# Where a fused RWKV-7 and feed-forward kernel begins its feed-forward, and who fetches its first weights

## The chip, the cores and the metric

The kernel runs on one NeuronCore of a Trainium2 chip. The core has five engines with a program each: TensorE (PE in the profile, its weight loads PEld), VectorE (DVE), ScalarE (ACT), GpSimd (POOL) and SyncE (SP). Each engine takes its instructions in the order of the program and waits on semaphores for the others. Transfers are issued by an instruction in the program of SP, ACT or POOL and are carried by 16 DMA engines that all of these share; an issuing instruction that has to wait (for a buffer, or for the data that it is to store) holds up everything behind it on its engine. The metric is the device time of one execution in microseconds, 1203.58 us before the change as the median of three runs (1201.11 to 1208.3).

## The reference, cut to what matters

```python
# r, k, v, w, a, b: (4 batches, 8 heads, 768 steps, 40), float32
for t in range(768):
    y[:, :, t] = einsum('bhd,bhde->bhe', r_t, state)
    Sa         = einsum('bhde,bhe->bhd', state, a_t)
    state      = state * w_t[:, :, None, :] - einsum('bhd,bhe->bhde', Sa, b_t)
    state      = state + einsum('bhd,bhe->bhde', v_t, k_t)
x = y.transpose(0, 2, 1, 3).reshape(3072, 320)
h = maximum(x @ w_in, 0)            # w_in  (320, 2048), float64
out = (h * h) @ w_out               # w_out (2048, 320), float64
```

The two feed-forward matrices come as float64. The kernel reads them as pairs of 32-bit words and makes float32 of them itself; that is called rounding below.

## The kernel before, in words

**Chunks and slots.** The 768 steps are cut into 6 chunks of 128 for each of 4 batches, 24 chunks in all, in the order of `order` (the four batches of one chunk in turn). The main loop (line 755) has one turn per chunk, called a slot here. Slot i interleaves, step by step (`weave`, 12 steps), up to five generators: `chain(i)`, the part of chunk i that depends on the state; `rest(i + 1)`, which turns and scales k, r, v, b of the next chunk; `prepare(m)` (`early`, with its loads) for a chunk 4 to 8 slots ahead, one or two of them in slots 0 to 15; 12 steps of the feed-forward `second`; and, in slots 0 to 3, some steps of `rounded`. The order in which these generators are stepped is the order of the program on every engine.

**The triangular solves.** `early` builds a triangular system per chunk and stores it to DRAM (`kept_q`, `kept_d`, `kept_n`, `kept_m`) together with the decays (`kept_e`, 780 KB). GpSimd solves the systems in units of two or four chunks: `solve(u)` loads a unit (`half_n`), takes 31 or 63 steps of a multiplication and a subtraction (lines 420 and 422), and stores the result (`kept_t`). `inverses(i)` reads the result back as T. For the first four chunks, whose systems are solved in halves, it also joins the halves: a transpose on DVE (line 454), small matmuls and copies in two steps. Chunk i of a unit cannot go through `chain(i)` before its unit is solved.

**Loads.** `load(i)` (line 148) issues, on SP's queue, the decays of the chunk (from slot 1 on) and then k, r, v and b, each 160 KB in pieces of 160 bytes. `load_early(i)` issues w, b and a for `early`. A store or a later load is put in `line` by `later(fn, steps)` and issued after so many steps.

**Rounding.** The raw words arrive in 21 fetches: 5 of 1 MB for `w_in` (two pieces of 512 columns each) and 16 of 320 KB for `w_out` (one piece each), 26 pieces in all. A piece takes two steps of `rounding`: two ACT operations (lines 257 and 261) and five DVE operations (lines 274 to 276, 265 and 266). The raw words lie where space is still unused: in `w_out` itself as long as it isn't filled (`wide`, `tails`), in the feed-forward's `hidden` (`lent`), and in two buffers of their own. `then` says after which piece which fetch is issued, on SP's queue; the first three (13 transfers) are issued on ACT's queue at line 711, right after the first solve.

**The feed-forward.** `ffn()` takes two chunks (256 tokens) as a group, 24 steps each. Eight pairs of blocks of 128 hidden units (16 steps, "in" below): for each block two 128-row matmuls and one 64-row matmul into `ps_f` (two buffers), then ACT's Relu (line 624) and DVE's product (line 625), which frees the buffer. Then 8 steps of four matmuls with `w_out` ("out"). A group's in steps wait for 10 finished pieces, its out steps for all 26. `share` says how many steps a slot runs before its chain and inside it: 6 before slot 2 and 2 inside, 8 inside slot 3, 4 before slot 4, 12 inside from slot 4 on. What is left after slot 23 runs alone at the end, 28 of 288 steps.

**Before the main loop** (lines 705 to 745, the prelude) the first two chunks are prepared and solved, chunks 2 and 3 prepared, chunk 0 taken through `rest`, and five pieces begun.

## Time and profile before

| | |
|---|---|
| median of three runs | 1203.58 us (1201.11 to 1208.3) |
| the profiled execution | 1197.18 us, span of its instructions 1195.5 us |
| busy share of the span | PE 85%, PEld 67%, DVE 40%, ACT 19%, POOL 57% |
| mean granted TensorE clock | 0.892 of full speed |
| moved by DMA | 114.38 MB in 260837 packets, 242828 of them under 512 B |
| queue of SP / of ACT / of POOL | 92.33 / 3.54 / 17.30 MB |

All times of a profile are microseconds from the start of the span of one profiled execution. In a timeline row the columns are start, duration, engine, source line, operation, output<-input, shape and count; the bracket at the end gives how long the engine had been idle and what ended that. SPq, ACTq and POOLq are the engines' own issuing of transfers. In a row of a table by stretches, each engine's busy time stands with its number of instructions, then the granted clock, the mean busy share of the DMA engines and GB/s.

### The profile page before, as it was taken

The numbers are of one execution on the slowest core, as the hardware profiler recorded it, in microseconds if no ns is written. First come the engines' busy times: TensorE is split into PE (matmuls) and PEld (weight loads), VectorE is DVE, ScalarE is ACT, GpSimd is POOL, SyncE is SP. The second block draws the span as 40 slices with busy tenths as digits, with TensorE's granted clock in tenths as the row PEclk, the third lists the DMA queues.
The fourth block names the chain that finished last, engine by engine and source line by source line (L and its number), as shares of the span: only waits on it lengthen the run. The fifth ranks groups of instructions, "written<-read, shape, count | busy, mean of one in ns | idle before, by whom it ended". The sixth has DMA issues, their size and how long they took to land.

```text
span 1195.5 us, 18978 instructions
## 1 busy us (share of the span) xinstructions
PE 1017.6 (85%) x7504; PEld 801.3 (67%) x7504; DVE 481.1 (40%) x1002; ACT 230.2 (19%) x535; POOL 683.7 (57%) x1112
## 2 busy tenths in 40 slices
PE   4248548858998999889979999879999999999898
PEld 3237446746776777667757777667777778777676
DVE  5347557636344246154144354142433132332211
ACT  2033222311121112112112112112122121221211
POOL 3753288458818866999279991179995881000000
PEclk9757557778999879979989989988999999999999
DMA  7894836372565947614565434544235433404000
GB/s 94 172 169 108 173 83 122 97 132 64 95 149 83 186 122 119 133 50 68 155 106 92 92 72 110 139 88 74 64 72 119 93 62 68 78 4 90 1 17 12
DMA packets 260837, 114.38 MB, mean 96 GB/s; under 512 B 242828, under 2 KB 248972, under 8 KB 258956
## 3 DMA queue, kind: packets, MB, share of 16 engines
q1 hardware_dynamic: 256476, 92.33, 39.9%
q0 software_dynamic: 2576, 17.30, 5.8%
q10 hardware_dynamic: 1696, 3.54, 1.3%
q8 instruction: 59, 0.97, 0.4%
q14 instruction: 30, 0.25, 0.1%
HBM read 76.42 MB, written 34.74 MB: 93 GB/s over the span
## 4 chain that ended last, share of the span: by engine, by line
PE 66%; DVE 13%; DMA 8%; SPq 7%; issue 3%; ACT 2%; ACTq 0%; DVEq 0%
PE ps_f L87 31%; PE ps_c L87 19%; PE ps_w L87 11%; SPq L142 4%; DMA in_k<-in_k_dram 3%; PE ps_w L314 3%; DVE decay L355 2%; SPq L108 2%; DVE hid L625 2%; DVE decay L356 2%; DMA in_w<-in_w_dram 1%; PE ps_w L512 1%; DVE RV L330 1%; PE ps_c L565 1%; ACT hid L624 1%
## 5 line engine op out<-in xcount | busy, mean ns | idle before, releaser
L420 POOL TENSOR_TENSOR half_p<-half_n,half_t 128x252 f32<-128x252 f32 (+52 forms) x503 | 306.7, 610 | 125.7 <-DMA half_n<-kept_d 66.7
L422 POOL TENSOR_TENSOR half_t<-half_t,half_p 128x252 f32<-128x252 f32 (+52 forms) x503 | 336.0, 668 | 39.4
L87 PE MATMUL ps_f<-tokens,w_in 128*128 128x256 f32 x704 | 206.1, 420 | 22.0 <-DVE hid L625 17.1
L87 PE MATMUL ps_f<-w_out,hid 128*128 128x320 f32 x704 | 205.7, 440 | 2.4 <-DVE hid L625 1.9
L87 PEld LDWEIGHTS ps_f<-w_out,hid 128*128 128x128 f32 x704 | 129.6, 192 | 52.3 <-DVE hid L625 4.9
L87 PEld LDWEIGHTS ps_f<-tokens,w_in 128*128 128x128 f32 x704 | 129.1, 203 | 49.1 <-DVE hid L625 27.1
L625 DVE TENSOR_TENSOR hid<-ps_f,hid 128x256 f32<-128x256 f32 x176 | 65.7, 414 | 238.0 <-ACT hid L624 238.0
L624 ACT ACTIVATE hid<-ps_f 128x256 f32<-128x256 f32 x176 | 57.9, 381 | 188.4 <-PE ps_f L87 188.3
L408 POOL DMA_DIRECT2D half_n<-kept_d x22 | 10.9, 500 | 121.3 <-DMA kept_d<-N 105.4
L488 DVE TENSOR_TENSOR kvT<-ps_w,dec 128x512 f32<-128x512 f32 x24 | 16.2, 675 | 126.8 <-PE ps_w L314 126.8
L87 PE MATMUL ps_f<-tokens,w_third 64*128 64x256 f32 x352 | 66.2, 455 | 0.0
L87 PEld LDWEIGHTS ps_c<-xr,T 64*64 64x64 f32 x768 | 53.2, 146 | 18.6 <-issue 16.7
L351 DVE TENSOR_TENSOR_SCAN decay<-ps_w,ones 128x64 f32<-128x64 f32 x88 | 23.5, 267 | 98.9 <-PE ps_w L314 98.9
L87 PE MATMUL ps_c<-xr,T 64*64 64x40 f32 x768 | 59.0, 238 | 1.1 <-ACT xr L547 1.0
L87 PEld LDWEIGHTS ps_c<-in_v,A 128*128 128x128 f32 x384 | 51.5, 210 | 2.7 <-issue 0.3
L87 PE MATMUL ps_w<-dec,kvT 40*128 40x128 f32 x384 | 35.1, 324 | 20.4 <-ACT N L367 11.8
L87 PE MATMUL ps_c<-in_v,A 128*128 128x40 f32 x384 | 50.4, 295 | 0.0
L87 PEld LDWEIGHTS ps_f<-tokens,w_third 64*128 64x128 f32 x352 | 28.3, 197 | 32.0 <-issue 31.0
L87 PE MATMUL ps_w<-rT,xnT 40*128 40x128 f32 x384 | 37.5, 320 | 14.3 <-DVE RV L330 13.5
L87 PEld LDWEIGHTS ps_w<-rT,xnT 40*128 40x128 f32 x384 | 30.8, 216 | 25.0 <-DVE RV L330 20.0
L87 PEld LDWEIGHTS ps_w<-dec,kvT 40*128 40x128 f32 x384 | 29.7, 221 | 25.5 <-ACT N L367 12.0
L367 ACT COPY N<-ps_w 128x512 f32<-128x512 f32 x48 | 25.8, 589 | 100.0 <-PE ps_w L87 60.5
(149 smaller groups left out, 1406.5 us busy)
## 6 DMA issues: line engine op xcount, KB each, us to landing
kept_e<-decay SPq DMA_DIRECT2D x22, 780.0 KB
dec<-kept_e SPq DMA_DIRECT2D x22, 780.0 KB
half_n<-kept_d POOLq DMA_DIRECT2D x16, 384.0 KB, 9.8
half_n<-kept_d POOLq DMA_DIRECT2D x6, 768.0 KB, 10.7
in_w<-in_w_dram SPq DMA_DIRECT2D x24, 160.0 KB
in_ab<-in_b_dram SPq DMA_DIRECT2D x24, 160.0 KB
in_ab<-in_a_dram SPq DMA_DIRECT2D x24, 160.0 KB
in_k<-in_k_dram SPq DMA_DIRECT2D x24, 160.0 KB
```

The source lines that it names most:

```text
L87: nc.tensor.matmul(o, l_, r_, start=start, stop=True, skip_group_check=True)
L108: later(lambda: queue.dma_start(out=out_, in_=in_), steps)
L142: nc.sync.dma_start(out=t_[:, :, :D], in_=src[bb, :, c * C:(c + 1) * C, :].rearrange("h t d -> t h d"))
L314: nc.tensor.transpose(p_[:, q * 128:(q + 1) * 128], pair(x_, q), ident)
L351: nc.vector.tensor_tensor_scan(up[:, q, MID + 1:C + 1], wT[:, q, MID:], ones, 1.0, Alu.mult, Alu.mult)
L355: nc.vector.reciprocal(down[:, :, MID + 1:C + 1], up[:, :, MID + 1:C + 1])
L356: nc.vector.reciprocal(up[:, :, :MID], down[:, :, :MID])
L367: nc.scalar.copy(t_[:, e * NP:(e + 1) * NP], p_)
L420: nc.gpsimd.tensor_tensor(p_, part[:, at:at + m_].unsqueeze(1).to_broadcast([128, n, m_]), t3[:, :n, s:s + 1].to_broadcast([128, n, m_]), ...
L422: nc.gpsimd.tensor_tensor(t3[:, :n, s + 1:], t3[:, :n, s + 1:], p_, Alu.subtract)
L624: nc.scalar.activation(h_, p_, Act.Relu)
L625: nc.vector.tensor_tensor(h_, p_, h_, Alu.mult)
```

## The change

Six things are altered.

1. The first three fetches of raw weights are issued by GpSimd instead of ACT: two ahead of its first solve, the third behind it.
2. Raw words of `w_out` lie in five places in turn (two own, three in `hidden`) instead of seven in a fixed list; `tails` goes, the list `then` is shorter, the first fetches of `w_out` are issued earlier and each later one when the piece that had its place is finished. A piece's `mant` and `bits` are both in PSUM (`ps_f`).
3. `load` issues k first, then the decays, then r; v and b follow two steps later.
4. `inverses` of a chunk is begun in `rest` where it was, but its joining steps are done at the end of `rest`; its two halves of small products lie in two PSUM tiles instead of one. In the prelude the joining of chunks 0 and 1 is begun right behind the second solve.
5. In a pair of blocks the two 64-row products come first, and a step ends after each block instead of after the first block's 128-row products and after the pair.
6. No feed-forward step runs in slots 0 to 3; 8 run before slot 4. Rounded pieces per slot are 4, 6, 6, 6 instead of 4, 8, 5, 5. After slot 23, 40 steps are left.

```diff
@@ -146,10 +146,12 @@
         early_loaded[i] = {nm: fetch(ring, src, i) for nm, ring, src in (("w", "w", w), ("b", "ab", b), ("a", "ab", a))}
 
     def load(i, g=None):
+        x_ = loaded[i] = {"k": fetch("k", k, i)}
         if g is not None:
             g["dec"] = new("dec", [128, 3, NP, C + 2], 2)
             nc.sync.dma_start(out=g["dec"], in_=kept_e[i])
-        loaded[i] = {nm: fetch(nm, src, i) for nm, src in (("k", k), ("r", r), ("v", v), ("b", b))}
+        x_["r"] = fetch("r", r, i)
+        later(lambda: x_.update(v=fetch("v", v, i), b=fetch("b", b, i)), 2 if g is not None else 0)
 
     load_early(0)
     load_early(1)
@@ -201,7 +203,6 @@
     lowest = single("lowest", [128, 1])
     nc.vector.memset(lowest, -896.0 * (1 << 23))
     wide = [room[:, 4 * WI * i:4 * WI * (i + 1)] for i in range(2)] + [free_words[:, :4 * WI]]
-    tails = [room[:, NF * DM - 2 * DM * (i + 1):NF * DM - 2 * DM * i] for i in range(2)]
     lent = [free_words[:, 2 * DM * i:2 * DM * (i + 1)] for i in range(3)]
     own_ = [single(f"raw{i}", [128, 2 * DM]) for i in range(2)]
 
@@ -228,14 +229,12 @@
               [w_third[:, WI * i:WI * (i + 1)] for i in range(2)])
     NARROW = len(pieces)
     WIDE = len(fetches)
-    in_turn = [own_[0], own_[1], tails[0], lent[0], lent[1], lent[2], tails[1], own_[0], own_[1], tails[0], tails[1],
-               own_[0], own_[1], own_[0], own_[1], own_[0]]
+    in_turn = [*own_, *lent]
     for f in range(NF):
-        fetchable(in_turn[f], [(0, 128, moe_w_out[f * 128:(f + 1) * 128, :])], [w_out[:, f, :]])
-
-    then = {0: (), 1: (3,), 3: (4,), 5: (5,), 6: (6,), 7: (8,), 8: (9,), 9: (7, 10)}
-    then.update({NARROW + n: tuple(WIDE + m_ for m_ in ms) for n, ms in
-                 ((0, (6, 7)), (1, (8,)), (2, (9,)), (6, (10,)), (7, (11,)), (8, (12,)), (11, (13,)), (12, (14,)), (13, (15,)))})
+        fetchable(in_turn[f % 5], [(0, 128, moe_w_out[f * 128:(f + 1) * 128, :])], [w_out[:, f, :]])
+
+    then = {0: (WIDE,), 1: (3,), 2: (WIDE + 1,), 3: (4,), 5: (WIDE + 2, WIDE + 3), 6: (WIDE + 4,)}
+    then.update({NARROW + f: (WIDE + f + 5,) for f in range(NF - 5)})
     finished = [0]
     left = lambda: len(pieces) - finished[0]
 
@@ -253,7 +252,7 @@
         for n in range(len(pieces) + 1):
             before, now = now, None
             if before:
-                _, _, _, bits = before
+                bits = before[-1]
                 nc.scalar.activation(bits, bits, Act.Relu, bias=lowest, scale=float(1 << 23))
             if n < len(pieces):
                 dst, raw = pieces[n]
@@ -268,9 +267,9 @@
                 for m_ in then.get(n - 1, ()):
                     later(lambda m_=m_: fetch_weights(m_, nc.sync), 1)
             if n < len(pieces):
-                hi, mant = words[:, :, 1].bitcast(I32), words[:, :, 0]
-                m_ = dst.shape[-1]
-                bits = (psum(ps_f)[:, :m_] if n < NARROW else new("bits", [128, DM], 1)).bitcast(I32)
+                hi = words[:, :, 1].bitcast(I32)
+                bits, mant = (psum(ps_f)[:, :dst.shape[-1]] for _ in range(2))
+                bits = bits.bitcast(I32)
                 nc.vector.tensor_scalar(bits, hi, 20, 0x7FF, Alu.logical_shift_right, Alu.bitwise_and)
                 nc.vector.tensor_scalar(mant.bitcast(I32), hi, 0xFFFFF, 0x100000, Alu.bitwise_and, Alu.bitwise_or)
                 nc.vector.tensor_tensor(mant, mant.bitcast(I32), dst, Alu.add)
@@ -454,20 +453,22 @@
         nc.vector.transpose(upper_.rearrange("p h t -> p (h t)"), blocks.rearrange("p h t -> p (h t)"))
         for n in range(2):
             nc.scalar.activation(T[:, :, n * Q:(n + 1) * Q], blocks, Act.Copy, scale=which[:, n:n + 1])
-        p_ = psum(ps_w).rearrange("p (n h t) -> p n h t", n=2, h=H)
+        small = lambda: psum(ps_w)[:, :H * Q].rearrange("p (h t) -> p h t", h=H)
+        p_ = small()
         mv = spare("mv", i)
         ends_ = [(slice(half * HC, half * HC + Q), slice(half * HC + Q, (half + 1) * HC)) for half in range(2)]
         for one, two in ends_:
             for h in range(H):
-                mm(p_[two, 0, h], g["joins"][one, h], upper_[one, h], True)
+                mm(p_[two, h], g["joins"][one, h], upper_[one, h], True)
         for one, two in ends_:
-            nc.scalar.copy(mv[two], p_[two, 0])
-        yield
+            nc.scalar.copy(mv[two], p_[two])
+        yield
+        p_ = small()
         for one, two in ends_:
             for h in range(H):
-                mm(p_[one, 1, h], mv[two, h], blocks[two, h], True)
+                mm(p_[one, h], mv[two, h], blocks[two, h], True)
         for one, two in ends_:
-            nc.scalar.copy(T[one, :, Q:], p_[one, 1])
+            nc.scalar.copy(T[one, :, Q:], p_[one])
         yield
 
 
@@ -487,11 +488,14 @@
         yield
         nc.vector.tensor_tensor(kT, kT_, down[:, :, 1:C + 1], Alu.mult)
         nc.vector.tensor_copy(ends, down[:, :, 0])
-        if soon(i) and i > 1:
-            yield from inverses(i, g)
+        joining = inverses(i, g) if i > 1 else iter(())
+        if soon(i):
+            next(joining, None)
         yield
         g["A"] = masked("A", 4, kT, aT)
         yield
+        while "v" not in x_:
+            line.pop(0)[1]()
         nc.scalar.copy(rT, turn(x_["r"]))
         vT = turned("kvT", 1)
         nc.scalar.copy(vT, turn(x_["v"]))
@@ -523,8 +527,7 @@
             sd = g["sd"] = new("sd", [128, NP, 2, DP], 2)
             nc.scalar.copy(sd.rearrange("p q e d -> p q (e d)"), quads(p_))
         yield
-        if not soon(i):
-            yield from inverses(i, g)
+        yield from joining
         yield
 
 
@@ -612,19 +615,16 @@
             for f in range(0, NF, 2):
                 ps = [psum(ps_f if gi < len(order) // GB - 1 else ps_w)[:, :GB * C] for _ in range(2)]
                 for e, p_ in enumerate(ps):
+                    half = slice(e * DP, (e + 1) * DP)
+                    mm(p_, w_third[half, f * 64:f * 64 + 128], t_[half, NT, :], True)
+                for e, p_ in enumerate(ps):
                     for j in range(NT):
-                        mm(p_, w_in[:, j, (f + e) * 128:(f + e + 1) * 128], t_[:, j, :], j == 0)
-                    if e == 0:
-                        yield True
-                for e, p_ in enumerate(ps):
-                    half = slice(e * DP, (e + 1) * DP)
-                    mm(p_, w_third[half, f * 64:f * 64 + 128], t_[half, NT, :], False)
-                for e, p_ in enumerate(ps):
+                        mm(p_, w_in[:, j, (f + e) * 128:(f + e + 1) * 128], t_[:, j, :], False)
                     h_ = hidden[:, (gi * NF + f + e) % (NF + 1)]
                     nc.scalar.activation(h_, p_, Act.Relu)
                     nc.vector.tensor_tensor(h_, p_, h_, Alu.mult)
                     hid.append(h_)
-                yield True
+                    yield True
             while left():
                 yield False
             for n in range(GB):
@@ -704,12 +704,15 @@
 
     run(firsts(0, 2))
     flush()
+    if moe_w_in.dtype != FP32:
+        for n in range(2):
+            fetch_weights(n, nc.gpsimd)
     solve(0, [nc.sync, nc.scalar])
     load_early(3)
     if moe_w_in.dtype != FP32:
-        for n in range(3):
-            fetch_weights(n, nc.scalar)
+        fetch_weights(2, nc.gpsimd)
     load(0)
+    flush()
     rounded = rounding() if moe_w_in.dtype != FP32 else as_they_are()
     e2, e3, r0 = early(2), early(3), rest(0, ready[0])
     go(e2, 3)
@@ -718,27 +721,27 @@
     go(r0, 3)
     flush()
     load(1)
+    flush()
     go(e3)
     go(r0)
     go(rounded, 2)
     go(e3, 2)
+    flush()
+    solve(1, own)
+    joined = [inverses(i, ready[i]) for i in range(2)]
+    go(joined[0])
+    go(joined[1])
     go(rounded)
     go(r0)
-    flush()
-    solve(1, own)
     go(rounded, 2)
     go(r0)
     go(rounded, 3)
-    tc.no_sync_barrier()
-    joined = [inverses(i, ready[i]) for i in range(2)]
-    go(joined[0])
-    go(joined[1])
     load_early(B)
     go(r0, 3)
-    go(rounded, 2)
     for _ in range(2):
         go(joined[0])
         go(joined[1])
+    go(rounded, 2)
     for gen in (e2, e3, r0, *joined):
         run(gen)
     flush()
@@ -748,8 +751,8 @@
     TOTAL = STEPS // GB
     ahead = {0: (4, 5), 1: (6,), 2: (7,), 3: (8,), 4: (9,), 5: (10, 11), 6: (12, 13), 7: (14, 15)}
     ahead.update({i: (i + 8,) for i in range(8, len(order) - 8)})
-    share = {0: (0, 0), 1: (0, 0), 2: (2, 6), 3: (8, 0), 4: (TOTAL, 4)}
-    pieces_in = {0: 4, 1: 8, 2: 5, 3: 5}
+    share = {**{i: (0, 0) for i in range(B)}, B: (TOTAL, 8)}
+    pieces_in = {0: 4, 1: 6, 2: 6, 3: 6}
     done = set(range(B))
     unit = FINE
     for i in range(len(order)):
```

## The prediction

> **What bounds the kernel now.** I read the chain of waits first, then a table of the engines by stretches, then the start of every slot, then single waits in the early slots.
>
> ```profile
> span 1195.5 us, 18978 instructions
> PE 66%; DVE 13%; DMA 8%; SPq 7%; issue 3%; ACT 2%; ACTq 0%; DVEq 0%
> ```
> ```profile
> 0.00:94.00 94.00, 38.48 (x306) 32.64 (x307) 42.81 (x85) 19.55 (x39) 51.87 (x151) 0.73 0.86 144
> 94.00:130.00 36.00, 27.19 (x240) 24.16 (x239) 32.46 (x62) 11.76 (x22) 8.01 (x22) 0.74 0.38 102
> 130.00:201.00 71.00, 40.25 (x311) 33.45 (x310) 37.54 (x68) 15.76 (x36) 53.39 (x94) 0.62 0.67 135
> 201.00:238.00 37.00, 33.38 (x291) 28.82 (x289) 26.30 (x52) 12.23 (x29) 20.99 (x44) 0.68 0.33 88
> 238.00:303.00 65.00, 47.20 (x307) 37.70 (x306) 30.63 (x61) 11.54 (x27) 49.13 (x88) 0.82 0.53 110
> 303.00:588.00 285.00, 264.42 (x1933) 208.31 (x1932) 121.71 (x258) 51.40 (x120) 205.85 (x316) 0.90 0.55 111
> 588.00:1118.00 530.00, 494.62 (x3761) 385.69 (x3759) 178.58 (x391) 96.56 (x233) 294.45 (x400) 0.97 0.41 84
> ```
>
> From 303 us on TensorE is busy for 264 of 285 and 495 of 530 us: there the kernel is bound by matrix work, which the change does not reduce. The first 303 us are another matter: PE works 38 of 94 us in the prelude and 148 of 209 in slots 0 to 3, at 0.62 to 0.82 of its clock, and the chain runs through DVE, DMA and SP's queue. So the change is decided there. I count a slot from its first copy into xr:
>
> ```profile
> 93.85 0.42 ACT L547 COPY xr<-ps_c 64x320 f32<-64x320 f32 x1 [2.77 <-PE ps_c L87]
> ...
> 129.10 0.42 ACT L547 COPY xr<-ps_c 64x320 f32<-64x320 f32 x1 [1.20 <-PE ps_c L87]
> ...
> 200.22 0.42 ACT L547 COPY xr<-ps_c 64x320 f32<-64x320 f32 x1 [1.26 <-PE ps_c L87]
> ...
> 236.95 0.42 ACT L547 COPY xr<-ps_c 64x320 f32<-64x320 f32 x1 [1.65 <-PE ps_c L87]
> ...
> 302.40 0.42 ACT L547 COPY xr<-ps_c 64x320 f32<-64x320 f32 x1 [4.37 <-PE ps_c L87]
> ...
> 587.56 0.42 ACT L547 COPY xr<-ps_c 64x320 f32<-64x320 f32 x1 [4.42 <-PE ps_c L87]
> ```
>
> Slots 0 to 3 take 35.3, 71.1, 36.7 and 65.5 us (208.6 in all); the last row is the start of slot 10. I forecast against the profiled execution's own time, 1197.2 us; the median of the runs lies 6.4 above it, and that is added at the end.
>
> **First weights by GpSimd; joining early (prelude).** The timeline, then the group of the solves' stores:
>
> ```profile
> 23.54 19.63 ACTq L248 DMA_DIRECT2D w_out<-in_moe_w_in_dram  x8
> ...
> 44.55 7.72 ACTq L248 DMA_DIRECT2D hid<-in_moe_w_in_dram  x5
> ...
> 52.37 1.07 ACT L367 COPY N<-ps_w 128x512 f32<-128x512 f32 x2 [30.29 <-DMA hid<-in_moe_w_in_dram]
> ...
> 53.01 2.56 PE L87 MATMUL ps_w<-dec,kvT 40*128 40x128 f32 x16 [11.78 <-ACT N L367]
> ...
> 81.83 0.66 ACT L261 ACTIVATE w_in<-hid 128x512 f32<-128x512 uint32 x1 [7.78 <-DMA hid<-kept_t]
> ```
> ```profile
> L425 POOL DMA_DIRECT2D kept_t<-half_t x9: 601/601/733, 55.7 to 990.5; - x9
> ...
> DMA to landing us min/median/max: 2.4/3.0/6.3
> ```
>
> ACT stands at its own 13 issues from 23.5 to 52.3, and PE waits 11.8 us for the copy behind them. With them gone the copies and all of rest and rounding behind them come 11.8 us earlier. What is late next is the solve: its result is stored at 55.7 us. On POOL the eight issues ahead of it take 0.6 us each by that row, 4.8 in all, inside the time in which POOL waits for the first systems; the 2 MB in flight slow these. I take 2 us (bounds 0 and 7.8, the longest wait for a load here). The third fetch, 5 issues or 3 us, stands ahead of the second solve, which nothing needs before slot 1 ends. So: 55.7 + 2 + 3.0 to land + 4.5 for reading the blocks back (bounds 2.4 and 7.8) = 65.2; from the landing at 81.8 to the first xr it is 12.0 us now, which stays; 2 us for rounded pieces that stand between. Slot 0 begins at 79 instead of 94: **-15** (bounds -22 and 0). SP meanwhile waits for the solve with the next raw fetches behind it; the five pieces begun before slot 0 are all in the first three fetches, so that wait costs nothing while slot 0 still has its 36 us to cover them.
>
> **Slots 0 to 3.** Three waits in them, and the k of two later slots:
>
> ```profile
> 144.27 1.12 PE L314 MATMUL ps_w<-ident,in_k 128*128 128x128 f32 x4 [9.86 <-DMA in_k<-in_k_dram]
> ...
> 157.70 1.70 PE L87 MATMUL ps_w<-hid 32*32 32x32 f32 x32 [8.77 <-DMA hid<-kept_m]
> ...
> 258.37 0.50 ACT L261 ACTIVATE w_out<-raw 128x320 f32<-128x320 uint32 x1 [14.36 <-DMA raw<-in_moe_w_out_dram]
> ...
> 604.04 1.09 PE L314 MATMUL ps_w<-ident,in_k 128*128 128x128 f32 x4 [7.18 <-DMA in_k<-in_k_dram]
> ...
> 781.29 1.09 PE L314 MATMUL ps_w<-ident,in_k 128*128 128x128 f32 x4 [6.75 <-DMA in_k<-in_k_dram]
> ```
>
> And what a feed-forward step and a rounded piece cost:
>
> ```profile
> 192.10 2.00 PE L87 MATMUL ps_f<-tokens,w_in 128*128 128x256 f32 x8 [0.92 <-DVE hid L625]
> 194.02 0.70 PE L87 MATMUL ps_f<-tokens,w_third 64*128 64x256 f32 x4
> ...
> 288.69 11.03 PE L87 MATMUL ps_f<-w_out,hid 128*128 128x320 f32 x40 [0.92 <-DVE hid L625]
> ...
> 1174.78 17.50 PE L87 MATMUL ps_w<-w_out,hid 128*128 128x320 f32 x64
> ```
> ```profile
> L276 DVE TENSOR_TENSOR raw<-raw,w_out 128x320 f32<-128x320 int32 x9 | 5.9, 660 | 0.3
> ...
> L274 DVE TENSOR_SCALAR ps_f<-w_out 128x512 int32<-128x512 int32 x8 | 5.5, 685 | 0.0
> L275 DVE TENSOR_SCALAR w_out<-w_out 128x512 int32<-128x512 int32 (+1 forms) x12 | 5.4, 448 | 0.1
> ```
>
> A pair of blocks with nothing else between is 2.00 + 0.70 + 0.92 = 3.6 us, 2.7 of it work; four out steps are 8.75 (half of 17.5). A piece is five DVE operations, by the first of the last three rows at most 3.3 us; I count half of it, since in these slots DVE is busy for half to nine tenths. The mant in PSUM: 685 against 448 ns at 512 columns bounds its loss at 0.24 us for one or two operations of 26 pieces, 6 to 12 us of DVE in all; but 660 ns for 320 columns in SBUF (first row), beside 685 for 512 columns into PSUM, say that SBUF is on average no cheaper per column. I take 0, and keep +6 and -6 for the range.
>
> - Slot 0: no row speaks for a change; 36.
> - Slot 1: 71.1, less three pairs ahead of slot 2 (10.9), the wait for k (9.9), the wait for the joins (8.8) and half of two pieces (3.3); plus 5 us, because the joining now stands at the end of rest with little to fill it (two products of 1.7 us, one transpose, two copies). 43. Bound above 55: if the wait for k only becomes one of DVE for the decays and that for the joins moves into the exposed end.
> - Slot 2: 36.7, less one pair (2.7), plus 5 and half a piece (1.7). 41.
> - Slot 3: 65.5, less the out steps ahead of slot 4 (11.0) and the wait for raw words (14.4), plus half a piece. 42; four pairs (10.8 of work) also go, which ran partly beside that wait, and I take 2 of them. 40. With five places each fetch is issued five pieces ahead, nearly a slot, which is why I let the wait go; bound 54 if it stays.
>
> Together 160 instead of 208.6: **-48.6** (bounds -58 and -21).
>
> **k ahead of decays, later.** In slots 10 and 14 (7.2 and 6.8 us) PE gets k first, but DVE then waits for the decays, which arrive no sooner, and the masked products behind need DVE. I take half: **-7** (0 to -13.9). v and b two steps later cost nothing while rest needs v only at its fifth step; if SP's queue is full then, PE waits for v where it waited for k, the upper bound. Elsewhere k is not waited for.
>
> **64-row products first.** The same matmuls; the second buffer is now needed only behind the first 64-row product, so of a 0.92 wait 0.35 is covered, in each pair where nothing else stands between. Some ten of these in the slots: **-3** (bounds -6 and +6, if a Relu and product per step disturb the copies of the chain).
>
> **Feed-forward moved.** Eight in steps ahead of slot 4: four pairs of 2.7 + 0.6 = **+13.2**. At the end 40 steps instead of 28: four pairs and four out steps, 13.2 + 8.75 = **+22.0**. What slots 0 to 3 lose of it stands in their sums.
>
> Sum: 1197.2 - 15 - 48.6 - 7 - 3 + 13.2 + 22.0 = 1158.8. With 6.4 up to the median: **1165 us**.
>
> **The solves as the next bound.** Slot 10 needs the sixth unit.
>
> ```profile
> 130.51 1.95 POOL L408 DMA_DIRECT2D half_n<-kept_d  x4 [26.64 <-DMA kept_d<-N]
> ...
> 573.26 0.60 POOL L425 DMA_DIRECT2D kept_t<-half_t  x1 [0.30 <-POOL half_t L422]
> ```
> ```profile
> POOL half_n L408 <- DMA kept_d<-N: 17.0, 2, 12.5
> POOL half_n L408 <- DMA kept_n<-N: 15.9, 1, 15.9
> ```
>
> From the first load to the result POOL needs 442.8 us, 32.9 of them waits for chunks that come earlier now: 409.9. It may begin 1.4 us after slot 1 (now 129.1), so at 79 + 36 + 1.4 = 116.4, and T of chunk 10 is there at 526.3 + 3.0 + some 3. My slot 10 begins at 587.6 - 50.4 (slot 4 at 252.0 instead of 302.4) - 2 = 535. It just fits; whatever slots 1 to 9 save beyond 3 us is not paid out unless slot 0 ends earlier too.
>
> **Rivals.**
> 1. *PE at half clock.* Slots 0 to 3 had 0.74, 0.62, 0.68 and 0.82. Without the feed-forward PE has 27.2, 32.2, 30.7 and 27.6 us of work there at these clocks; at 0.50 this is 40, 40, 42 and 45, 167 instead of my 160, and some 6 us of waits beside it: +13, **1178**. For it speaks that the clock was highest in slot 3, which had most feed-forward; against it, that slot 2 ran in 37 us at 0.68 with one pair. The Trainium skill, "TensorE: Matmul & The Clock Gate", in "Why this matters for your kernels", says that a pause of some 3 us between bursts sends PE back to half clock; the waits of 8 to 14 us above and the clocks beside them agree.
> 2. *Transfers bound the prelude.* In its 94 us the DMA engines are busy for 0.86, and the change takes no byte from it; 2 MB run beside the first systems. If slot 0 begins at 94 as before: +15, **1180**. Against it: the ACT wait is an issue and not data. The Trainium skill, "DMA: Bandwidth & Descriptors", "Issuing engines are not separate DMA queues", holds that another issuer saves only issue time, usually little; here that time was 27 us, so the row differs in size.
> 3. *The feed-forward was free filler.* If DVE and transfers, not PE, set the length of slots 0 to 3, they lose only what stood alone ahead of slots 2 and 4 (10.9 + 11.0), and the prelude gains nothing: 1197.2 - 21.9 + 13.2 + 22.0 + 6.4 = **1217**, slower. It decides as soon as prelude and slots save less than the 35 us added elsewhere. For it: DVE is 32 of 36 us busy in slot 0. Against it: the three waits of slots 1 and 3 are 33 us alone.
> 4. *More goes than I count*: k in full, slots at 36 to 40, prelude at its lower bound: some -17, **1148**.
>
> **How the numbers follow.** Forecast 0.45, rivals 0.20, 0.17, 0.08 and 0.10. About 0.5%, 6 us, is what a measurement of this kernel can tell from no change. Only rival 3 ends above; with the upper bounds of the unknown costs piling up on rivals 1 and 2 I give slower 0.07, same 0.05, faster 0.88. The range goes from below rival 4 to beyond rivals 1 and 2 with their bounds: 1141 to 1195.
>
> **What would show it.** Right: ACT without a 30 us wait before its first copies of chunk 2; slot 0 at 75 to 85; slot 1 near 43; no wait for in_k over 4 us; no ACT wait for raw in slot 3; slot 4 at 245 to 260; some 22 us more of feed-forward alone at the end. Wrong: slot 0 near 94 (rival 2), granted clocks of 0.5 in slots 1 to 3 with PE busy throughout (rival 1), DVE busy throughout at the old lengths (rival 3), or PE waiting for T at slot 10 (the solves).

## The result, and the profile after

The changed kernel takes 1167.55 us (median of 4 runs, 1163.86 to 1179.45), the kernel before beside it 1205.94 (1201.11 to 1209.4): ratio 0.9701, 95% interval 0.9621 to 0.9782. The forecast was 1165. The profiled execution took 1165.97 us. Its span and its chain of waits, from the page of the changed kernel:

```profile
span 1164.3 us, 19023 instructions
...
PE 66%; POOL 11%; DVE 8%; DMA 8%; SPq 3%; issue 3%; ACT 2%; DVEq 0%; POOLq 0%; ACTq 0%
```

POOL was not among the engines of this line before and now holds 11% of the chain; SP's queue fell from 7 to 3%. The table by stretches of the changed kernel, cut at the first copy into xr of each slot: prelude, slots 0, 1, 2, 3, and then slots 4 to 9, slot 10, and what follows slot 23's begin.

```profile
0.00:85.50 85.50, 36.42 (x304) 31.09 (x304) 42.52 (x84) 19.56 (x39) 49.95 (x146) 0.61 0.90 146
85.50:123.69 38.19, 27.41 (x236) 24.41 (x236) 33.49 (x61) 11.48 (x22) 14.78 (x39) 0.72 0.66 150
123.69:167.98 44.29, 36.54 (x272) 32.55 (x272) 28.40 (x60) 12.13 (x28) 28.25 (x59) 0.50 0.65 142
167.98:212.08 44.10, 34.71 (x272) 30.84 (x272) 26.08 (x57) 12.08 (x28) 38.99 (x66) 0.58 0.52 124
212.08:264.73 52.65, 45.71 (x277) 36.60 (x278) 27.16 (x61) 12.48 (x29) 37.89 (x79) 0.74 0.70 151
```
```profile
264.73:521.83 257.10, 248.48 (x1933) 196.54 (x1933) 123.84 (x258) 54.19 (x121) 214.19 (x324) 0.98 0.52 114
521.83:583.04 61.21, 46.02 (x309) 35.60 (x308) 16.87 (x36) 8.11 (x18) 37.40 (x60) 0.80 0.63 138
1063.02:1164.27 101.25, 96.09 (x452) 65.37 (x450) 15.56 (x35) 16.68 (x42) 0.00 (x0) 1.00 0.03 10
```

Set against the same cuts of the kernel before, with what the prediction's steps made of each part:

| part | before | after | difference | forecast |
|---|---|---|---|---|
| prelude | 93.85 | 85.50 | -8.4 | -15 |
| slots 0 to 3 | 208.55 | 179.23 | -29.3 | -35.4 |
| slots 4 to 9 | 285.15 | 257.10 | -28.1 | about -1 |
| slots 10 to 22 | 529.7 | 541.2 | +11.5 | about -9 |
| slot 23 and what follows | 78.24 | 101.25 | +23.0 | +22.0 |
| span | 1195.5 | 1164.3 | -31.2 | -38.4 |

(The forecast for slots 0 to 3 has the eight steps ahead of slot 4 in it, -48.6 + 13.2; tenths that do not add up are rounding.) The span misses the forecast by 7 us; the median agrees to 2.6, since the medians moved by 36 to 38 where these two executions differ by 31. And the 7 are a sum of errors that cancel: 28 us came from slots 4 to 9, where almost nothing was forecast, and slots 10 to 22 gave 11.5 back, where 9 were to be gained. That the whole came so near is in part luck.

The row of slots 4 to 9 is read beside that of the kernel before (303 to 588 us in the prediction): the same 1933 matmuls take 248.5 us of PE's time instead of 264.4, at a clock of 0.98 instead of 0.90, and PE stands for 8.6 us instead of 20.6. What slot 10 gave back is one wait. PE's and POOL's timelines of the changed kernel:

```profile
528.94 0.60 POOL L424 DMA_DIRECT2D kept_t<-half_t  x1 [0.30 <-POOL half_t L421]
...
536.79 1.90 PE L87 MATMUL ps_c<-xr,T 64*64 64x40 f32 x16 [14.15 <-DMA T<-kept_t]
```

POOL issues the store of unit 5's result at 528.9 us, PE has it at 536.8 and had nothing else for 14.15 us: the next bound, which the prediction had judged to "just fit". In the prelude, the engines' timelines:

```profile
10.67 4.19 POOL L247 DMA_DIRECT2D w_out<-in_moe_w_in_dram  x8
...
14.68 13.23 SPq L108 DMA_DIRECT2D kept_q<-N  x4
...
34.28 0.24 POOL L419 TENSOR_TENSOR half_p<-half_n,half_t 128x31 f32<-128x31 f32 x1 [18.55 <-DMA half_n<-kept_q]
...
61.71 0.62 POOL L424 DMA_DIRECT2D kept_t<-half_t  x1 [0.30 <-POOL half_t L421]
...
64.11 2.69 SPq L441 DMA_DIRECT2D hid<-kept_t  x4
...
75.61 0.87 DVE L453 STREAM_TRANSPOSE hid<-hid 128x256 f32<-128x256 f32 x2 [8.08 <-DMA hid<-kept_t]
```

The weights are issued ahead of the first solve, whose result is stored at 61.7 us instead of 55.7 (SP's stores of its systems, `kept_q`, take until 27.9 us); the four reads of the blocks begin at 64.1 and have landed at 75.6, 11.5 us later, where 4.5 were counted.

### The profile page after: what moved, and what is told of

The parts are those of the page before. It is cut to its first block, busy times and chain, and to the rows that moved or that the text cites. A ratio compares the mean times of both kernels' runs of the same rounds, so it can differ in the third digit from the quotient of the medians.

```text
span 1164.3 us, 19023 instructions
## 1 busy us (share of the span) xinstructions
PE 1037.0 (89%) x7504; PEld 816.3 (70%) x7504; DVE 477.7 (41%) x1002; ACT 241.2 (21%) x535; POOL 685.5 (59%) x1125
## 4 chain that ended last, share of the span: by engine, by line
PE 66%; POOL 11%; DVE 8%; DMA 8%; SPq 3%; issue 3%; ACT 2%; DVEq 0%; POOLq 0%; ACTq 0%
PE ps_f L87 30%; PE ps_c L87 19%; PE ps_w L87 11%; POOL half_t L421 6%; POOL half_p L419 5%; PE ps_w L313 3%; DMA in_w<-in_w_dram 3%; DVE decay L354 1%; PE ps_w L516 1%; DVE decay L355 1%; DMA kept_q<-N 1%; DMA dec<-kept_e 1%; SPq L142 1%; DMA half_n<-kept_d 1%; DVE RV L329 1%
## 5 line engine op out<-in xcount | busy, mean ns | idle before, releaser
L625 DVE TENSOR_TENSOR hid<-ps_f,hid 128x256 f32<-128x256 f32 x176 | 73.8, 419 | 364.4 <-ACT hid L624 364.0
L87 PE MATMUL ps_f<-tokens,w_in 128*128 128x256 f32 x704 | 200.4, 412 | 0.0
L87 PEld LDWEIGHTS ps_f<-tokens,w_in 128*128 128x128 f32 x704 | 124.9, 196 | 44.0 <-issue 30.8
L624 ACT ACTIVATE hid<-ps_f 128x256 f32<-128x256 f32 x176 | 67.6, 384 | 271.6 <-PE ps_f L87 271.1
L87 PE MATMUL ps_f<-tokens,w_third 64*128 64x256 f32 x352 | 85.6, 430 | 6.5 <-DVE hid L625 4.7
L87 PEld LDWEIGHTS ps_c<-xr,T 64*64 64x64 f32 x768 | 54.8, 150 | 35.4 <-issue 28.9
L87 PEld LDWEIGHTS ps_f<-tokens,w_third 64*128 64x128 f32 x352 | 39.4, 191 | 33.4 <-DVE hid L625 22.1
L350 DVE TENSOR_TENSOR_SCAN decay<-ps_w,ones 128x64 f32<-128x64 f32 x88 | 23.6, 268 | 88.5 <-PE ps_w L313 77.4
L528 ACT COPY sd<-ps_c 128x512 f32<-128x512 f32 x20 | 11.7, 587 | 153.5 <-PE ps_c L526 153.5
L597 DVE TENSOR_TENSOR tokens<-ps_c,dec 128x512 f32<-128x512 f32 x24 | 16.6, 692 | 62.5 <-PE ps_c L87 62.5
L87 PE MATMUL ps_w<-decay,bT 40*128 40x128 f32 x352 | 28.9, 310 | 12.4 <-DVE decay L359 9.3
```

The source lines that it names most:

```text
L87: nc.tensor.matmul(o, l_, r_, start=start, stop=True, skip_group_check=True)
L350: nc.vector.tensor_tensor_scan(up[:, q, MID + 1:C + 1], wT[:, q, MID:], ones, 1.0, Alu.mult, Alu.mult)
L528: nc.scalar.copy(sd.rearrange("p q e d -> p q (e d)"), quads(p_))
L597: nc.vector.tensor_tensor(t_, y_, g["up"][:, :, :C], Alu.mult)
L624: nc.scalar.activation(h_, p_, Act.Relu)
L625: nc.vector.tensor_tensor(h_, p_, h_, Alu.mult)
```

## The experiments

All ratios are against the kernel before on the same chip; the times of the places are from one profiled execution each. The last column but two is the time from the begin of slot 1 to that of slot 11. In the two kernels with eight steps ahead of slot 10 these steps lie in slots 4 to 9, so no figure stands there.

| kernel | median, us | ratio (95%) | slot 0 at | slots 0-3 | slots 4-9 | slot 1 to 11 | PE's wait for chunk 10's T | from slot 23 |
|---|---|---|---|---|---|---|---|---|
| before | - | 1 | 93.9 | 208.6 | 285.2 | 508.3 | - | 78.2 |
| changed | 1167.55 | 0.9701 (0.9621-0.9782) | 85.5 | 179.2 | 257.1 | 459.3 | 14.15 | 101.3 |
| before + part 5 | 1209.81 | 1.0013 (0.9981-1.0046) | 94.0 | 220.4 | 281.4 | 519.4 | - | 76.4 |
| before + part 3 | 1196.09 | 0.9881 (0.9822-0.9939) | 95.0 | 217.4 | 275.1 | 504.8 | - | 78.2 |
| changed - parts 2, 6 | 1177.02 | 0.9735 (0.9674-0.9797) | 89.2 | 216.8 | 267.4 | 498.5 | 4.65 | 76.7 |
| changed, unit 5 short | 1149.76 | 0.9497 (0.9437-0.9556) | 85.7 | 187.0 | 252.4 | 441.5 | 0.40 | 101.3 |
| changed - part 1 | 1159.42 | 0.9609 (0.9526-0.9692) | 85.1 | 183.0 | 257.4 | 457.5 | 14.32 | 100.9 |
| changed, weights by SP | 1161.41 | 0.9638 (0.9568-0.9708) | 77.4 | 185.8 | 259.7 | 459.7 | 13.78 | 100.9 |
| changed - part 4 in slots | 1185.99 | 0.9831 (0.9752-0.9910) | 85.9 | 202.9 | 257.7 | 475.4 | 12.27 | 101.2 |
| changed - part 5 | 1174.13 | 0.9723 (0.9632-0.9814) | 85.0 | 177.5 | 274.7 | 464.2 | 1.23 | 101.3 |
| changed, again | 1165.75 | 0.9635 (0.9590-0.9680) | 85.5 | 177.6 | 257.1 | 458.0 | 14.09 | 101.3 |
| changed + 8 steps ahead of slot 10 | 1143.25 | 0.9449 (0.9403-0.9495) | 84.7 | 186.7 | - | 458.1 | 0.98 | 84.2 |
| the same - part 1 | 1136.07 | 0.9392 (0.9347-0.9436) | 85.8 | 177.5 | - | 458.9 | none | 83.9 |
| changed - part 3 | 1190.61 | 0.9844 (0.9794-0.9894) | 85.8 | 184.7 | 258.8 | 470.2 | 14.13 | 101.2 |

### Two parts alone, in the kernel before

The question of the first two was which part had given the 28 us of slots 4 to 9. The order within a pair, alone:

```diff
                 for e, p_ in enumerate(ps):
-                    for j in range(NT):
-                        mm(p_, w_in[:, j, (f + e) * 128:(f + e + 1) * 128], t_[:, j, :], j == 0)
-                    if e == 0:
-                        yield True
-                for e, p_ in enumerate(ps):
                     half = slice(e * DP, (e + 1) * DP)
-                    mm(p_, w_third[half, f * 64:f * 64 + 128], t_[half, NT, :], False)
+                    mm(p_, w_third[half, f * 64:f * 64 + 128], t_[half, NT, :], True)
+                for e, p_ in enumerate(ps):
+                    for j in range(NT):
+                        mm(p_, w_in[:, j, (f + e) * 128:(f + e + 1) * 128], t_[:, j, :], False)
...
-                yield True
+                    yield True
```

> The kernel before with one part of the change: the two 64-row products first in a pair of blocks, and a step after each block. In the changed kernel slots 4 to 9 (first copy into xr of slot 4 to that of slot 10) take 257.1 us where they took 285.2, which the prediction did not hold. Theory P, the pair: the waits for the feed-forward buffer and the half-clock stretches behind them go with this part; then slots 4 to 9 take 255 to 268 us here and the whole is 15 to 30 us shorter. Rival L, the loads: this part alone leaves slots 4 to 9 at 280 or more and the whole within 6 us. Rival S, the shift of the feed-forward against the slots: the same as L here.

Measured: 1.0013, and slots 4 to 9 took 281.4 instead of 285.2. The order alone is worth nothing that shows. The loads alone (the first added line stands ahead of the decays):

```diff
-        loaded[i] = {nm: fetch(nm, src, i) for nm, src in (("k", k), ("r", r), ("v", v), ("b", b))}
+        x_ = loaded[i] = {"k": fetch("k", k, i)}
...
+        x_["r"] = fetch("r", r, i)
+        later(lambda: x_.update(v=fetch("v", v, i), b=fetch("b", b, i)), 2 if g is not None else 0)
...
```

> The kernel before with k loaded ahead of the decays and v and b two steps later, nothing else. Rival L (the order of the loads frees SP's queue and with it the waits in slots 4 to 9): slots 4 to 9 fall from 285 to 255 to 268 us. Theory P and rival S: they stay at 280 or more. All: no wait of PE for in_k over 4 us is left (9.9, 7.2 and 6.8 us before); of these 24 us the prediction's step gives half, some 7 us in slots 10 and 14 and up to 9.9 in slot 1, so 5 to 17 us of the whole.

Measured: 0.9881, 10 us less in slots 4 to 9, which lies between what the theories had said (255 to 268 us, or 280 and more; it is 275.1). But the waits for k in slots 10 and 14 are mostly handed on. PE's timeline of this kernel:

```profile
607.48 0.80 PE L87 MATMUL ps_w<-dec,kvT 40*128 40x128 f32 x4 [6.01 <-DVE kvT L490]
...
791.08 1.15 PE L87 MATMUL ps_w<-dec,kvT 40*128 40x128 f32 x10 [4.33 <-DVE kvT L490]
```

Where PE had waited 7.2 and 6.8 us for k it now waits 6.0 and 4.3 for DVE's kT, which needs the decays: a quarter saved of what the prediction halved.

### The feed-forward and the raw words as before

The old list of places, the old `then`, `mant` outside PSUM, and the old `share` and `pieces_in` in the changed kernel:

```diff
...
-    share = {**{i: (0, 0) for i in range(B)}, B: (TOTAL, 8)}
-    pieces_in = {0: 4, 1: 6, 2: 6, 3: 6}
+    share = {0: (0, 0), 1: (0, 0), 2: (2, 6), 3: (8, 0), 4: (TOTAL, 4)}
+    pieces_in = {0: 4, 1: 8, 2: 5, 3: 5}
```

> The changed kernel with the feed-forward back in slots 2 and 3, 6 steps ahead of slot 2 and 4 ahead of slot 4, and with it the old places, order and numbers of the rounded pieces, which it needs. Rival S (the feed-forward's groups lie differently against the slots): slots 4 to 9 go back to 280 us or more. Theory P and rival L: they stay at 250 to 262. By the prediction's ledger the moved steps cost 35 us where they go and save 27 us in slots 1 to 3, and the wait for raw words (14.4 us) comes back: slot 4 begins 10 to 25 us later, the tail is 22 us shorter, and the whole is within 10 us of the changed kernel. If the feed-forward was free filler in slots 2 and 3, the whole is 15 us or more shorter than the changed kernel.

Measured: 0.9735. By parts 2 and 6 slots 0 to 3 get 37.6 us shorter (216.8 to 179.2), slots 4 to 9 10 us shorter, and the end 24.5 longer. At 267.4 us slots 4 to 9 lie between what rival S and the two other theories had said, and slot 4 begins 41 us later, more than the 10 to 25 expected. The whole is the same as with them within the intervals: what they free before slot 10 is lost in slot 10 and at the end.

### Half of unit 5's solve

This kernel leaves out half of the steps of unit 5, so T of chunks 10 to 13 is not the true one.

```diff
-        for s in range(size - 1):
+        for s in range((size - 1) // 2 if u == 5 else size - 1):
```

> The changed kernel with half of the steps of the sixth unit's solve left out (31 of 63), so that chunks 10 to 13 get a wrong T; nothing else is left out. In the changed kernel PE stands 14.15 us in slot 10 for T of chunk 10, GpSimd having solved without a pause from 125 to 529 us. If the solves are the bound there, as the prediction's last step had it, the wait is gone, slot 10 takes 42 to 48 us instead of 61.2, and the whole is 13 to 20 us shorter: 13 or 14 if only the wait is paid, 17 to 20 if the half-clock stretch that follows it (24 us long) is paid as well. If the wait only hides another one behind it (SP's queue, the loads of chunk 11), less than 8 us is gained.

Two rows of it, POOL's timeline and the table by stretches for slot 10:

```profile
476.47 0.60 POOL L424 DMA_DIRECT2D kept_t<-half_t  x1 [0.30 <-POOL half_t L421]
```
```profile
525.09:572.30 47.21, 41.92 (x309) 32.74 (x308) 16.90 (x36) 8.12 (x18) 29.52 (x44) 0.96 0.75 152
```

The result is stored at 476.5 us and slot 10 takes 47.2 us instead of 61.2, though slots 0 to 3 happened to be 8 us longer in this execution. The same 309 matmuls need 4.1 us less of PE, at a clock of 0.96 instead of 0.80. By the ratios the whole gains 17 to 25 us against the changed kernel (0.9497 beside 0.9635 and 0.9701), more than the 14 of the wait. The solve of chunks 10 to 13 is shown to bound the changed kernel.

### Who issues the first weights

ScalarE again, behind the first solve:

```diff
-        for n in range(2):
-            fetch_weights(n, nc.gpsimd)
     solve(0, [nc.sync, nc.scalar])
...
-        fetch_weights(2, nc.gpsimd)
+        for n in range(3):
+            fetch_weights(n, nc.scalar)
```

> The changed kernel with part 1 alone undone: the first three fetches are issued by ScalarE behind the first solve again; the early start of the joining (part 4) stays. Theory A, ScalarE's 13 issues were the price in the prelude: ScalarE stands from about 24 to 52 us, everything behind its copies comes some 8 us later, slot 0 begins at 92 to 95 instead of 85.5, T of chunk 10 comes 8 us later, and the whole is 8 to 12 us longer (ratio to before 0.978 to 0.981). Theory B, the gain came from the joining being begun earlier, and GpSimd's issues cost what ScalarE's did: the first solve is stored at about 56 us again instead of 61.7, slot 0 begins at 80 to 87, and the whole is within 4 us of the changed kernel (0.967 to 0.974).

```profile
14.71 6.77 SPq L108 DMA_DIRECT2D kept_q<-N  x4
...
48.69 2.65 ACTq L247 DMA_DIRECT2D hid<-in_moe_w_in_dram  x5
...
55.72 0.73 POOL L424 DMA_DIRECT2D kept_t<-half_t  x1 [0.30 <-POOL half_t L421]
...
66.97 2.69 SPq L441 DMA_DIRECT2D hid<-kept_t  x4
...
75.17 0.76 DVE L453 STREAM_TRANSPOSE hid<-hid 128x256 f32<-128x256 f32 x2
...
85.05 0.42 ACT L550 COPY xr<-ps_c 64x320 f32<-64x320 f32 x1 [1.38 <-PE ps_c L87]
```

Theory A falls. ACT is held until 51.3 us as before, and slot 0 begins at 85.05, as with GpSimd's issues. What decides is when DVE transposes the blocks: slot 0 begins 9.9 us behind that here, in the changed kernel and in the next one (10.1 in the kernel before, 83.7 to 93.9). Here the blocks are read from 67.0 us on and ACT uses them at 71.7, but DVE comes to them at 75.2 without a pause, from the rounding and the rest that ACT's 13 issues made late. In the changed kernel DVE is through with these at 67.5 and waits 8.1 us for the blocks, until 75.6. So with GpSimd the work behind ACT comes 7.7 us earlier, but the solve is stored 6.0 us later and its blocks take 11.5 us to read instead of 4.7; the two waits end at the same time and cancel. GpSimd's own issuing ends at 14.9 us and is not what delays the solve: with the weights in flight SP's stores of the systems take 13.2 us instead of 6.8 (the rows with `kept_q<-N` here and in the prelude's view above).

By exclusion the 8 us of the prelude come from part 4, the joining begun right behind the second solve, and some of them from the raw words: slot 0 begins at 85.0 to 85.9 us with part 1, 3, 5 or the joining in the slots undone, at 89.2 without parts 2 and 6. No run undoes the joining in the prelude by itself.

The third issuer, SyncE, with two fetches behind the loads of chunk 0 and the third behind those of the blocks:

```diff
-        fetch_weights(2, nc.gpsimd)
     load(0)
+        for n in range(2):
+            fetch_weights(n, nc.sync)
...
     go(joined[1])
+        fetch_weights(2, nc.sync)
```

> The changed kernel with the first three fetches issued by SyncE: two behind the first chunk's k, r, v and b, the third behind the loads of the joined blocks; neither ScalarE nor GpSimd issues any. Theory B (GpSimd's eight issues ahead of its stores and of its first solve cost 6 us): the first solve is stored at 54 to 57 us instead of 61.7, slot 0 begins at 76 to 80 instead of 85.5, slot 1 and the run of solves behind it 6 to 9 us earlier, T of chunk 10 likewise, and the whole is 6 to 10 us shorter than the changed kernel (ratio to before 0.962 to 0.965). Rival, 2 MB of transfers and not the issuer delay the small stores and loads: slot 0 at 84 to 88, ratio 0.968 to 0.973.

```profile
55.19 0.73 POOL L424 DMA_DIRECT2D kept_t<-half_t  x1 [0.31 <-POOL half_t L421]
...
60.89 2.68 SPq L441 DMA_DIRECT2D hid<-kept_t  x4
...
67.51 0.43 DVE L453 STREAM_TRANSPOSE hid<-hid 128x256 f32<-128x256 f32 x1
...
85.39 1.08 PE L313 MATMUL ps_w<-ident,in_w 128*128 128x128 f32 x4 [8.04 <-DMA in_w<-in_w_dram]
...
122.65 0.42 ACT L550 COPY xr<-ps_c 64x320 f32<-64x320 f32 x1 [1.35 <-PE ps_c L87]
```

And PE's row of the same load in the changed kernel:

```profile
87.61 1.09 PE L313 MATMUL ps_w<-ident,in_w 128*128 128x128 f32 x4 [2.15 <-DMA in_w<-in_w_dram]
```

Slot 0 begins 8 us earlier, at 77.4, as expected, but then takes 45.3 us, and slot 1 begins at 122.7, 1.0 before the changed kernel. In this slot PE waits 8.0 us for in_w, a load that stands on SP's queue behind raw weights (issued at 75.3 us). The wait is not made by this issuer: in the changed kernel the load is issued at 76.7, also behind raw weights, and is used at 87.6; the earlier slot 0 only stands longer in front of it. So T of chunk 10 comes no earlier. The whole (0.9638) can't be told from the changed kernel; the gain of the prelude was not paid out.

### The joining in the middle of rest

```diff
-        joining = inverses(i, g) if i > 1 else iter(())
-        if soon(i):
-            next(joining, None)
+        if soon(i) and i > 1:
+            yield from inverses(i, g)
...
```

> The changed kernel with the joining in the slots done in the middle of rest again, where it was before (the prelude stays as changed). If the wait for the halves (8.8 us in slot 1 before) was what the late joining removed, it is back with nothing else to fill it: slots 1 and 2 take 47 to 54 us each instead of 44.3 and 44.1, and slot 10 begins 5 to 15 us later; but T of chunk 10 does not come later, so the 14 us wait there shrinks by as much and the whole stays within 4 us of the changed kernel (ratio to before 0.967 to 0.974). If the joining at the end of rest costs more than it removes (I had put 5 us on it in each of two slots), slots 1 and 2 take 38 to 42 us and the whole again stays, with a longer wait in slot 10.

PE's timeline of this kernel in slots 1, 2 and 3, and below it the one small product of slot 1 in the changed kernel:

```profile
153.23 1.73 PE L87 MATMUL ps_w<-hid 32*32 32x32 f32 x32 [12.02 <-DVE hid L453]
...
201.18 1.72 PE L87 MATMUL ps_w<-hid 32*32 32x32 f32 x32 [9.91 <-DVE hid L453]
...
240.79 1.09 PE L313 MATMUL ps_w<-ident,in_k 128*128 128x128 f32 x4 [9.38 <-DMA in_k<-in_k_dram]
```
```profile
159.02 1.70 PE L87 MATMUL ps_w<-hid 32*32 32x32 f32 x32 [1.99 <-issue]
```

The waits come back (12.0 and 9.9 us for the transposes, which wait for the blocks; 2.0 in the changed kernel), and slots 0 to 3 take 202.9 us instead of 179.2. But 7.2 of these 23.7 us lie in slot 0, which the edit does not touch (the last section has its two lengths). Slots 1 and 2 grow by 2.7 and 3.8 us, to 47.0 and 47.9, and slot 3 by 10.0, where PE waits 9.4 us for k; why k is late there is not shown. My expectation for slots 1 and 2 was near; that for the whole failed: 0.9831 instead of 0.970. T of chunk 10 did not stay where it was, because longer early slots also store the systems later: POOL had to wait 13.5 us (5.9 and 7.6) for systems within its long run, and stored T 420.2 us after slot 1 began instead of 405.3. From slot 1 to slot 11 the late joining is worth 16 to 17 us, about 1.5%.

### The order of the pair and the loads, undone in the changed kernel

Part 5 alone undone (the reverse of the first diff):

> The changed kernel with part 5 alone undone (128-row products first, a step ends after the first block's 128-row products). Part 5 alone in the kernel before gave 3.8 us in slots 4 to 9 and nothing in the whole. Theory S, from slot 1 to slot 10 the solves set the time: if slots 4 to 9 get longer (257.1 now; 260 to 275), the wait of 14 us for T of chunk 10 gets shorter by the same amount, slot 11 begins at 581 to 586 as now (583.0), and the whole changes by less than 4 us (ratio 0.967 to 0.974). Rival, the order of the pair is what keeps TensorE free of short waits in slots 4 to 9 when the loads are early: slots 4 to 9 take 270 to 285 and the whole gets longer by 6 to 15 us (0.975 to 0.983).

Stretch and timeline rows:

```profile
262.39:537.12 274.73, 259.47 (x1933) 203.51 (x1933) 123.10 (x258) 51.16 (x120) 222.42 (x341) 0.93 0.52 111
```
```profile
528.74 0.60 POOL L424 DMA_DIRECT2D kept_t<-half_t  x1 [0.30 <-POOL half_t L421]
...
539.80 1.09 PE L87 MATMUL ps_c<-xr,T 64*64 64x40 f32 x16 [1.23 <-DMA T<-kept_t]
```

Each theory is right in one place. Slots 4 to 9 grow by 17.6 us (11.0 of busy time at a clock of 0.93, 6.6 of idle), as the rival had it; but T comes at the same time as in the changed kernel (528.74 beside 528.94), so that the wait for it shrinks from 14.15 to 1.23 and slot 11 begins 5 us later, not 18. The order that gave 4 us in the kernel before gives 17.6 here, and 12.9 of them only lengthen the standing in front of T. In the whole (0.9723) no difference from the changed kernel is shown. Part 3 alone undone, beside the changed kernel itself:

> The changed kernel as it is, beside the three others on one chip. Ratio to before 0.966 to 0.974, the wait for T of chunk 10 again 13 to 15 us, slot 0 at 85 to 86.

Measured: 0.9635, just below what was expected, with slot 0 at 85.5 us and the wait at 14.1.

> The changed kernel with part 3 alone undone: the decays first, then k, r, v and b together. Part 3 alone in the kernel before shortened slots 4 to 9 by 10 us. Theory S with the loads: slots 4 to 9 take 264 to 272 us instead of 257.1, the wait for T of chunk 10 shrinks by as much (to 0 to 7 us), a wait for in_k of 4 to 8 us stands in slot 14 again, and the whole is 3 to 10 us longer than the changed kernel (ratio 0.972 to 0.980). Rival, the early loads matter only where the order of the pair is old: slots 4 to 9 stay at 255 to 260 and the whole within 3 us.

```profile
270.46:529.25 258.79, 250.73 (x1933) 197.32 (x1933) 123.42 (x258) 54.10 (x121) 215.75 (x326) 0.97 0.54 114
```
```profile
544.19 1.90 PE L87 MATMUL ps_c<-xr,T 64*64 64x40 f32 x16 [14.13 <-DMA T<-kept_t]
...
559.46 0.90 PE L311 MATMUL ps_w<-ident,in_k 128*128 128x128 f32 x3 [5.30 <-DMA in_k<-in_k_dram]
...
747.48 0.90 PE L311 MATMUL ps_w<-ident,in_k 128*128 128x128 f32 x3 [10.78 <-DMA in_k<-in_k_dram]
```

What I expected of the place is wrong and of the whole too small. Slots 4 to 9 do not notice (258.8), and the wait for T stays at 14.1: slot 1 began 7.5 us later here than in the changed kernel beside it, and slot 10 and T with it. The loss lies in slots 10 and 14, where k is awaited for 5.3 and 10.8 us; the stretch of slots 10 to 15 takes 304.3 us beside 286.7. The whole, 1190.6 beside 1165.75 us, loses 2.1%, about twice what part 3 gave alone in the kernel before. So the 28 us of slots 4 to 9 belong to no single part: the order of the pair with the shifted feed-forward carries them, and the loads carry some of them only where these two are old.

### The wait filled with feed-forward

If in slot 10 the kernel waits for POOL and not for PE, steps of the feed-forward that would stand at the end cost nothing there:

```diff
-    share = {**{i: (0, 0) for i in range(B)}, B: (TOTAL, 8)}
+    share = {**{i: (0, 0) for i in range(B)}, B: (TOTAL, 8), 10: (TOTAL, 8)}
```

> The changed kernel with eight steps of the feed-forward put ahead of the chain of slot 10, as eight already stand ahead of slot 4; so 32 instead of 40 are left after slot 23. Theory S, in slot 10 TensorE has nothing to do for 14 us because T of chunk 10 comes from GpSimd at 536.8 us whatever TensorE does: the first copy of slot 10 comes some 13 us later (535 instead of 521.8), the wait for T is 0 to 2 us, slot 11 begins within 3 us of 583, and the end alone gets 13 us shorter (88 instead of 101.25); the half clock behind the wait goes too. Whole 11 to 18 us less than the changed kernel (ratio to before 0.955 to 0.961). Rival, the wait is not TensorE's to fill (DVE, the gathering of tokens or SyncE's queue is what is late in slot 10): slot 11 begins 8 to 13 us later than 583, and the whole is within 4 us of the changed kernel.

```profile
538.41 0.60 POOL L424 DMA_DIRECT2D kept_t<-half_t  x1 [0.30 <-POOL half_t L421]
...
546.37 0.80 PE L87 MATMUL ps_c<-xr,T 64*64 64x40 f32 x11 [0.98 <-DMA T<-kept_t]
```
```profile
546.37:588.37 42.00, 40.91 (x309) 31.84 (x310) 16.27 (x34) 7.34 (x17) 24.87 (x39) 1.00 0.76 168
1052.15:1136.37 84.22, 79.71 (x396) 55.33 (x395) 13.45 (x30) 14.30 (x36) 0.00 (x0) 0.99 0.03 10
```

The wait is 0.98 us, what follows runs at full clock, the end is 17.0 us shorter, and slot 11 begins 458.1 us behind slot 1, beside 458.0 in the changed kernel on this chip: the eight steps cost nothing. The whole is 22.5 us shorter (1143.25 beside 1165.75), more than I had expected; slots 11 to 22 are 18 us shorter too, 11 of them in the same matmuls, at a clock of 1.00 instead of 0.97, and 7 in PE's idle time. Why that is so is not shown. And with ScalarE as the issuer:

> The same eight steps ahead of slot 10, and the first three fetches issued by ScalarE again (part 1 undone). If the issuer decides nothing, as the earlier run of part 1 undone says, this is within 4 us of the kernel with the eight steps alone. If ScalarE is the better issuer, as that run's time alone would suggest (0.9609 beside 0.9701), it is 6 to 12 us shorter than that. Ratio to before 0.950 to 0.962.

Measured: 1136.07 us, 0.9392, 7 us less than with GpSimd, which is what was to speak for ScalarE. The ratios' intervals overlap (0.9347 to 0.9436 and 0.9403 to 0.9495), but the six times of each kernel on this chip differ by 6.1 us in the mean, with a 95% interval of 1 to 11. The profiles do not say where it comes from: slot 0 is 9.7 us shorter in this one, but one kernel's slot 0 has both lengths (last section), and slot 11 begins 458.9 us behind slot 1 beside 458.1. Part 1 brought no gain in either comparison and seems to cost about half a per cent; the cause stays open. This last kernel is the best of all, 2.5% below the changed one on the same chip.

## Why the prediction was right, and where it was not

**What bounds the kernel.** That the first 303 us decide held only for their own 38 us. Slots 4 to 9 counted as matrix work that the change does not reduce; but their idle time fell by 12 us and the same matmuls took 16 us less. A busy PE at 0.90 of its clock was slack, and I had the 0.90 in the quoted row.

**First weights by GpSimd; joining early: -15, measured -8.4.** The bounds (-22 and 0) held it. The copies behind ACT's issues did come 10.7 us earlier (chunk 2's at 41.6 us instead of 52.4), and rest and rounding with them. The step that failed is the next one, "55.7 + 2 + 3.0 to land + 4.5 for reading the blocks back", 65.2 in all: the blocks were there at 75.6. Two of its terms were mis-sized: the delay of the solve was 6.0 (I took 2, bound 7.8), the reading of the blocks 11.5 (4.5, bound 7.8, passed). The last part, 12.0 + 2, was 9.9. Rival 2's price, slot 0 at 94, did not come, but its mechanism did: the 2 MB beside the first systems are what delays the solve. The Trainium skill, "DMA: Bandwidth & Descriptors", "Issuing engines are not separate DMA queues", holds that another issuer saves only issue time, usually little; between ScalarE and GpSimd the work behind that time came 7.7 us earlier here, which is not little, and was lost in the wait for the blocks. The three issuers, which also issue at different times, gave slot 0 at 85.1, 85.5 and 77.4, and slot 1 within 3.5 us.

**Slots 0 to 3: 173.2 with the steps ahead of slot 4, measured 179.2** (177.6 in the second execution). 38.2, 44.3, 44.1 and 52.7 us beside 36, 43, 41 and 53.2. The waits for the joins and for raw words went as said. The joining at the end of rest did pay. Slots 1 and 2, 4.4 us over, ran at granted clocks of 0.50 and 0.58: that fits rival 1, at less than half of its price of 13, but no run separates the clock from the other causes there. One reading in the sum was off: the 11.0 us of out steps ahead of slot 4 are five steps (x40 in the row), and four are 8.75 by the prediction's own figure.

**k ahead of decays: -7.** Alone in the kernel before, PE's two waits lost 3.6 us. The changed kernel without it is 25 us longer, only partly by the waits of 5.3 and 10.8 us. The term was too small, and its place (slots 10 and 14) right.

**64-row products first: -3.** None alone (1.0013), 17.6 us in slots 4 to 9 within the change. A pair standing alone costs 3.55 us after (two pairs at the end begin at 1092.22 and 1095.77) beside 3.6, so nearly nothing of the covered 0.35 us showed. I had priced this wait and not what short waits do to the clock.

**Tail +22, measured +23.0**, and the eight steps ahead of slot 4 as counted.

**The solves as the next bound.** The mechanism and its place were right and "just fits" was not: T was stored at 528.9 us (526.3 in the prediction), and PE had it at 536.8 where 532.3 was reckoned: 2.6 us later in the store and 1.9 more on the way. But slot 10 came at 521.8 instead of 535 because of the unforecast 28 us. The sentence that what slots 1 to 9 save beyond 3 us is not paid out describes the result: in the changed kernel, again, with either other issuer, and in both kernels with filled slot 10, slot 11 begins 457.5 to 459.7 us behind slot 1. T of chunk 10 is stored 404.6 to 408.1 us behind slot 1 in these and in the kernels with part 3 or 5 undone. PE waiting for T at slot 10 was named as a sign of being wrong, and it came; of the signs of being right, slot 0 (85.5 for 75 to 85) and slot 4 (264.7 for 245 to 260) just missed.

**Rival 3** was half right: by the run with old feed-forward and raw words, parts 2 and 6 change the whole by no more than the intervals. By the runs that undo them, the kernel got faster by the joining (about 1.5%) and the loads (2.1%), with the moved feed-forward neutral.

## What to carry to other kernels

When one engine runs a long serial job beside the main work, its finishing time is a schedule of its own: write it beside the main one, and put work that can wait (here what stands alone at the end) in front of the place where the main work must meet it. A change on a path that ends in such a meeting is to be tested with the meeting removed, else its gain or loss disappears in the wait. And price a short pause of PE with the clock behind it, not by its own length.
